# Attention and a gated feed-forward in one planned kernel: the weight loads behind the first forty go in single file

## The chip, the cores and the metric

The kernel runs on one core of a Trainium2 chip. The metric is the device time of one execution in microseconds (us); times are given as the median of the executions shown.

## What is computed

The reference has two parts, and the second reads the first's output.

```
B, H, S, D = 8, 8, 576, 64                       # attention, for every batch b and head h
q_d, k_d, v_d = means of q, k, v over groups of 4 positions      # 144 positions
out_up    = repeat(softmax(q_d k_d^T / 8) v_d, 4 times each)
out_local = softmax(q k^T / 8, only where |i - j| < 4) v
x = (out_up + out_local) as 4608 tokens x 512
h = x @ w_in            # 512 x 2048
y = (h * cos(h)) @ w_out    # 2048 x 512
```

All data is float32 at the interface. The weights come as 64-bit floats and are turned into pairs of 32-bit floats (a high and a low part) on the chip.

## The kernel before

**Work and tiles.** Attention is done in units of one batch and two heads: b0 to b7, four units each. A unit has loads of q and k (`u_qk`, L478) and of v in two layouts, vd and vl (`u_v`, L498), then scores and softmax (`u_s`), transposes (`u_t`) and the product with v (`u_pv`), which writes one of four ring slots of x tiles (x0 to x3). The feed-forward goes over 12 tiles of 384 tokens and 16 slices of 128 of the inner width. A step is one tile and one slice: `gemm1` (L946, 12 matmuls at L969 of 384 columns), an epilogue on ACT, DVE and POOL (L978 to L987) and, two steps later, `gemm2` (L991, nine matmuls at L1005 of 512 columns). The epilogue holds one of two PSUM banks until its second pass on DVE (L984) is through. The first three tiles go through the slices in three passes: slices 0 to 3, then 4 to 7, then 8 to 15, three tiles in each; the other nine tiles go through all 16 slices at once. Steps are numbered from 0 in that order: steps 0 to 11 are the first pass, 12 to 23 the second, 24 to 47 the third. So slice 4 is first needed at step 12, and slice 15 at step 31.

**Weights.** For each slice there are two loads of 512 KB: wdi (a slice of w_in) and wdo (a slice of w_out), made by `w_load` (L407) on SP's queue. A loaded slice is split (`w_split`, L417): an absolute value on ACT (L425), four passes on DVE (L426 to L432), a cast to the high part on ACT or DVE (L436, L437) and a subtraction on POOL or DVE (L404). The buffers of slices 6 to 15 hold data of the first attention units before that (names beginning with wxi and wxo), so those loads wait until the units are through.

**What sets the order.** Every operation is recorded in a plan with an engine, a cost and its dependencies; some have a choice of engines. A list scheduler (`Plan.run`, L163) goes over the recorded operations eight times forwards and backwards with priorities, keeps the best outcome, and the operations are then issued to each engine's in-order queue in the order of their planned starts. The loads of the first units and of all weights are tied to one order (L1069 to L1072). A load's planned cost is its size by a rate on SP and 1.8 more until it is there (L396). The planner also puts fillers into TensorE's order before 300 us of its plan (L1131: a 128x512 matmul on a constant, into an unused bank), where it expects TensorE to wait or to be too little busy.

**Loads in flight.** `dma` (L388) gives each of the first forty transfers on SP's queue (FIRST = 40) a wait for the transfer three ahead of it (AHEAD = 3), so that three are in flight. Behind the fortieth there is no such wait. Each SP transfer uses one of eight semaphores in turn (DMAHW0 to DMAHW7), and waits for the earlier transfer with the same one; besides, it waits for the engines that use its buffer. SP's queue also carries the output stores of the first three tiles' first passes (L1027) and small moves of softmax results (ptb, L854), all in order. An output store reads a buffer ob, which shares a ring of four with the epilogue's tiles tr.

Of the kernel before, what the change touches and what calls it, by code (L numbers as in the profile page):

```python
# [24 lines left out]
P = 128  # L25
# [9 lines left out]
NF = 4  # L35
# [15 lines left out]
ON_PE = ()  # L51
BOOST = {0: 100.0}
LAG = 2
AHEAD, FIRST = 3, 40
PI = math.pi


# [223 lines left out]
def _mmr(n, k=1):  # L281
    return k * n * 0.0004543
# [6 lines left out]
def _act(n, psum=True, extra=0):  # L289
    return n * 0.000833 + (0.051 if psum else 0.093) + 0.093 * extra  # L290


def _dve(n):
    return n * 0.001042 + 0.065
# [7 lines left out]
def attn_ffn_kernel(ctx: ExitStack, tc: tile.TileContext, qT, kT, vdn, vl, w_in, w_out, out):  # L302
    nc = tc.nc
    pe, act, dve, pool, sp = nc.tensor, nc.scalar, nc.vector, nc.gpsimd, nc.sync
# [6 lines left out]
    pl = Plan()  # L311

    def sb(tag, n, shape, dtype=F32, name=None, pool=None):
        t = pl.turn(tag, n)
        return pl.buf(lambda: (pool or ap).tile(shape, dtype, name=name or tag, tag=t, bufs=1), t)

    def psum(tag):
        pl.banks.append((tag, pl.buf(lambda: ps.tile([P, 512], F32, name="bank", tag=tag, bufs=1), tag)))
        return pl.banks[-1][1]
# [65 lines left out]

    loads, begun = {}, []

    def dma(nbytes, fn, r=(), w=(), pw=()):  # L388
        def begin():
            ins = fn()  # L390
            if ins is not None and len(begun) < FIRST:
                if len(begun) >= AHEAD:
                    tc.add_manual_dep(ins.ins, begun[-AHEAD].name, mybir.DependencyInfo(
                        mybir.DependencyClass.Sync, mybir.DependencyReason.DATA), reason="loads in flight")
                begun.append(ins.ins)
        o = pl.op("SP", max(0.45, nbytes / 262e3), begin, r=r, w=w, pw=pw, lat=1.8)  # L396
        loads.setdefault((pl.name,) + pl.arg, []).append(o)
        return o

# [7 lines left out]
    def w_load(k, c):  # L407
        pl.name = "w_load"
        wd = words[(k, c)]
        if k == "i":  # L410
            src = lambda: w_dram["i"][:, :, c * P:(c + 1) * P, :]
            dst = lambda: wd.get().rearrange("p (a f) t -> p a f t", a=KC)
        else:
            src, dst = (lambda: w_dram["o"][c * P:(c + 1) * P]), wd.get
        dma(4096 * P, lambda: sp.dma_start(dst(), src()), w=[wd])
# [535 lines left out]
    def pe_order(o):  # L951

        if prev[0] is not None:
            o.sdeps.append(prev[0])
        prev[0] = o
# [35 lines left out]
    po, part = {}, {}  # L991

    def gemm2(t, c, c0, c1):
        pl.name = "gemm2"
        gh, gl = gt.pop((t, c))
        if c == c0:
            po[t] = [psum(f"po.{i}") for i in range(SIZE[t] // P)]
        wo, accs = wgt[("o", c)], po[t]
        end = (t, c) == (NT - 1, NC - 1)

        def mm(i, lo, hi):
            sl = slice(i * P, (i + 1) * P)
            o = accs[i].get()
            for k in range(lo, hi):
                pe.matmul(o, (gh, gh, gl)[k].get()[:, sl], wo.get()[:, (0, 1, 0)[k]], start=(c == c0 and k == 0),  # L1005
                          stop=(c == c1 - 1 and k == 2))

        def high(i):
            pe_order(pl.op("PE", 2 * _mmr(DM), lambda: mm(i, 0, 2), r=[gh, wo], w=[accs[i]]))
        if end:  # L1010
            high(0)
            high(1)
        for i in range(SIZE[t] // P):
            lo = 2 if end else 0
            if end and i == 2:
                high(2)
            pe_order(pl.op("PE", (3 - lo) * _mmr(DM), lambda i=i: mm(i, lo, 3), r=[gh, gl, wo], w=[accs[i]]))
            if c == c1 - 1:
                bk, ob = accs[i], sb("tr", 4, [P, DM], name="ob", pool=fp)

                pl.op("ACT", _act(DM), lambda bk=bk, ob=ob: act.activation(ob.get(), bk.get(), AF.Copy, scale=-4.0 * PI),
                      r=[bk], w=[ob], alts=[("DVE", _dve(DM), lambda bk=bk, ob=ob: dve.tensor_scalar(
                          out=ob.get(), in0=bk.get(), scalar1=-4.0 * PI, scalar2=None, op0=ALU.mult))])
                dst = out[FROM[t] + i * P:FROM[t] + (i + 1) * P, :]
                if c0 == 0:
                    part[(t, i)] = pl.buf(None)
                    dma(2048 * P, lambda dst=dst, ob=ob: sp.dma_start(dst, ob.get()), r=[ob], w=[part[(t, i)]])  # L1027
                else:

                    pl.op("POOL", 1.0, lambda dst=dst, ob=ob: pool.dma_start(dst, ob.get(), accum_op=ALU.add),  # L1030
                          r=[ob], w=[part[(t, i)]], lat=2.5)
# [22 lines left out]
    for c in range(NC):  # L1054
        for k, d in (("i", 0.0), ("o", 0.7)):
            t = need[c]
# [73 lines left out]
    def wide(s):  # L1130
        return pe.matmul(s[2].get(), ident_b, ident_b.unsqueeze(1).broadcast_to([P, 4, P]), start=True, stop=True)  # L1131
# [5 lines left out]
    with tc.manual_schedule():  # L1137
        constants()
        for o in order:
            if o.eng == "PE" and o.start < CFG["fend"]:  # L1140
# [3 lines left out]
                if s:  # L1144
# [5 lines left out]
                    for (x, d), (y, _) in zip(marks, marks[1:] + [(o.start - 0.2, None)]):  # L1150
                        n = int((y - x) * CFG["fill"] / 0.22)
                        if y > o.start - 0.3:
                            n = max(n, least)
                        for i in range(n):
                            ins = wide(s)
# [51 lines left out]
```

## Time and profile before

| | us |
|---|---|
| three timed executions | 999.63, 1001.82, 1000.99 |
| their median | 1000.99 |
| the profiled execution, whole | 1007.59 |
| its span, first to last instruction | 1005.80 |
| TensorE busy in it | 988.6 |
| VectorE busy in it | 677.0 |
| ScalarE busy in it | 612.3 |
| mean share of the DMA engines | 0.27 of the span |

The profiled execution lies 6.60 us above the median of the timed ones; 1.79 us of it lie outside the span. In the profile's rows PE is TensorE's matmul side, DVE is VectorE, ACT is ScalarE, POOL is GpSimd, and SPq is the queue of SyncE. A row of the timeline has its start, its length, engine, line, operation, tiles and count, and in square brackets the idle time before it and what ended it. A window row has the stretch, then for PE, PEld, DVE, ACT and POOL the busy time and the instructions, then TensorE's granted clock, the DMA engines' share and GB/s.

### The profile page before, as it was taken

To read this page: it belongs to the slowest core of one execution; us is meant where nothing else is said; L and a number is where in the kernel's file an instruction comes from. 1 tells how busy PE (TensorE), PEld (TensorE's weight loads), DVE (VectorE), ACT (ScalarE), POOL (GpSimd) and SP (SyncE) were. 2 spreads that over 40 slices of the span, in tenths; PEclk is the share of its full clock that TensorE was granted. 3 is DMA by queue.
4 is the path that set the end of the run, shared out by engine and by line. 5 is a ranking of instruction groups with operands and counts; after the bars stand their busy time and mean duration, and the time that the engine had idled before them with its cause. 6 is when DMAs were issued, how large, how long until landed. Compare 5 with 4: busy or idle time off the path is not lost.

```text
span 1005.8 us, 24165 instructions
## 1 busy us (share of the span) xinstructions
PE 988.6 (98%) x10081; PEld 858.6 (85%) x10081; DVE 677.0 (67%) x1418; ACT 612.3 (61%) x1175; POOL 185.6 (18%) x250
## 2 busy tenths in 40 slices
PE   7999999999999999999999999999999999999998
PEld 4767888998888888889888888888888888899997
DVE  5489989997778668464758867655657875433433
ACT  2349868886567656555547756655646755655554
POOL 3257325352232103000002111100001200000000
PEclk9599999999999999999999999999999999999999
DMA  7861663224243412210212412201112320100000
GB/s 233 251 216 38 222 236 98 43 33 92 61 104 96 92 50 72 67 33 28 80 50 69 129 49 57 83 25 37 62 54 72 113 63 3 38 1 1 32 1 32
DMA packets 39756, 78.36 MB, mean 78 GB/s; under 512 B 4832, under 2 KB 16096, under 8 KB 39648
## 3 DMA queue, kind: packets, MB, share of 16 engines
q1 hardware_dynamic: 37056, 72.11, 22.9%
q0 software_dynamic: 2592, 4.72, 3.3%
q8 instruction: 79, 1.29, 0.5%
q14 instruction: 29, 0.24, 0.1%
HBM read 57.93 MB, written 14.16 MB: 72 GB/s over the span
## 4 chain that ended last, share of the span: by engine, by line
PE 89%; DVE 4%; issue 3%; DMA 2%; ACT 1%; SPq 1%; POOL 0%; ACTq 0%; DVEq 0%; POOLq 0%
PE bank L969 37%; PE bank L1005 37%; PE bank L1131 2%; PE bank L731 2%; PE bank L914 2%; PE bank L750 2%; PE bank L895 1%; PE bank L890 1%; PE bank L867 1%; DMA q<-qT 1%; PE bank L907 1%; DMA ptb<-sml 1%; PE bank L864 1%; PE bank L676 1%; SPq L854 1%
## 5 line engine op out<-in xcount | busy, mean ns | idle before, releaser
L1005 PE MATMUL bank<-wo,gh 128*128 128x512 f32 x1152 | 364.3, 397 | 0.0
L1005 PEld LDWEIGHTS bank<-wo,gh 128*128 128x128 f32 x1152 | 209.4, 188 | 38.3 <-issue 3.6
L1005 PE MATMUL bank<-wo,gl 128*128 128x512 f32 x576 | 227.5, 395 | 0.0
L980 ACT ACTIVATE tr<-bank,bmagic 128x384 f32<-128x384 f32 x192 | 111.0, 578 | 108.7 <-PE bank L969 104.0
L984 DVE SCALAR_TENSOR_TENSOR tr<-tr,bank 128x384 f32<-128x384 f32 x192 | 105.0, 547 | 105.2 <-ACT tr L979 104.3
L981 DVE SCALAR_TENSOR_TENSOR tr<-tr,bank 128x384 f32<-128x384 f32 x192 | 105.5, 550 | 82.5 <-ACT tr L980 81.3
L978 ACT ACTIVATE tr<-tr 128x384 f32<-128x384 f32 x192 | 100.5, 523 | 81.8 <-DVE tr L981 81.3
L986 ACT ACTIVATE gh<-tr 128x384 fp32r<-128x384 f32 x160 | 83.7, 523 | 88.2 <-DVE tr L984 86.7
L404 DVE TENSOR_TENSOR gl<-tr,gh 128x384 fp32r<-128x384 f32 x159 | 95.5, 601 | 57.9 <-ACT gh L986 55.6
L1005 PEld LDWEIGHTS bank<-wo,gl 128*128 128x128 f32 x576 | 108.0, 188 | 23.5
L969 PE MATMUL bank<-x1h,wi 128*128 128x384 f32 x384 | 107.4, 340 | 0.8 <-DVE tr L984 0.8
L969 PE MATMUL bank<-x0h,wi 128*128 128x384 f32 x384 | 107.0, 339 | 0.0
L969 PE MATMUL bank<-x2h,wi 128*128 128x384 f32 x384 | 106.8, 339 | 0.0
L969 PE MATMUL bank<-x3h,wi 128*128 128x384 f32 x384 | 106.5, 338 | 0.0
L979 ACT ACTIVATE tr<-tr 128x384 f32<-128x384 f32 x192 | 100.9, 525 | 6.1
L404 POOL TENSOR_TENSOR gl<-tr,gh 128x384 fp32r<-128x384 f32 x33 | 38.4, 1165 | 233.2 <-DVE gh L987 150.2
L969 PEld LDWEIGHTS bank<-x1h,wi 128*128 128x128 f32 x384 | 70.2, 188 | 3.7 <-DVE tr L984 1.6
L969 PEld LDWEIGHTS bank<-x0h,wi 128*128 128x128 f32 x384 | 70.2, 188 | 2.1
L969 PEld LDWEIGHTS bank<-x2h,wi 128*128 128x128 f32 x384 | 70.2, 188 | 2.0 <-issue 0.2
L969 PEld LDWEIGHTS bank<-x3h,wi 128*128 128x128 f32 x384 | 70.2, 188 | 2.0
L969 PE MATMUL bank<-x3l,wi 128*128 128x384 f32 x192 | 64.5, 336 | 0.0
L969 PE MATMUL bank<-x0l,wi 128*128 128x384 f32 x192 | 64.5, 336 | 0.0
(277 smaller groups left out, 1436.7 us busy)
## 6 DMA issues: line engine op xcount, KB each, us to landing
vl<-vl SPq DMA_DIRECT2D x26, 384.0 KB, 3.0
out<-ob SPq DMA_DIRECT2D x36, 256.0 KB, 2.1
wdi<-w_in SPq DMA_DIRECT2D x16, 512.0 KB, 10.2
wdo<-w_out SPq DMA_DIRECT2D x16, 512.0 KB, 6.8
q<-qT SPq DMA_DIRECT2D x26, 292.0 KB, 3.5
k<-kT SPq DMA_DIRECT2D x26, 292.0 KB, 3.1
vd<-vdn SPq DMA_DIRECT2D x26, 288.0 KB
out<-ob POOLq DMA_DIRECT2D x18, 256.0 KB, 5.0
```

The costliest lines, as they stand in the source:

```text
L404: f = lambda e: lambda: e.tensor_tensor(out=out(), in0=in0(), in1=in1(), op=ALU.subtract)
L731: pe.matmul(banks[h].get()[BS * g:BS * (g + 1), c:c + BS], q.get()[hs, o:o + BS], k.get()[hs, o:o + BS], start=True, stop=True)
L750: pe.matmul(banks[h].get()[:HD, i * SD:(i + 1) * SD], qkd.get()[hs, 0, i * HD:(i + 1) * HD], qkd.get()[hs, 1, :], start=True, stop=True)
L914: pe.matmul(banks[e].get()[64 * h:64 * h + 64, o:o + 2 * BQ], v4[r, NSEG * h + n, :], pt[r, :, NSEG * h + n, :BQ], start=True, stop=True)
L969: pe.matmul(ph.get()[:, :m], w[:, i, kc, :], x[:, kc, :], start=(n == 0), stop=(n == 3 * KC - 1))
L978: act.activation(tr.get(), tr.get(), AF.Sin, scale=PI)
L979: return act.activation(tr.get(), tr.get(), AF.Square)
L980: pl.op("ACT", _act(m, True, 1), lambda: act.activation(tr.get(), h(), AF.Identity, bias=bmagic), r=[ph], w=[tr])
L981: pl.op("DVE", _dve(m), lambda: dve.scalar_tensor_tensor(out=tr.get(), in0=tr.get(), scalar=MAGIC, in1=h(), op0=ALU.subtract, op1=ALU.subt ...
L984: pl.op("DVE", _dve(m), lambda: dve.scalar_tensor_tensor(out=tr.get(), in0=tr.get(), scalar=0.5, in1=h(), op0=ALU.subtract, op1=ALU.mult), ...
L986: pl.op("ACT", _act(m, False), lambda: act.activation(gh.get(), tr.get(), AF.Copy), r=[tr], w=[gh], alts=[("DVE", _dve(m / 2), lambda: dve ...
L1005: pe.matmul(o, (gh, gh, gl)[k].get()[:, sl], wo.get()[:, (0, 1, 0)[k]], start=(c == c0 and k == 0), stop=(c == c1 - 1 and k == 2))
```

## The change

Loads 41 to 80 on SP's queue now wait for the one load directly ahead of them, in place of none; output stores are neither counted nor given a wait, and no load waits for them. In the planner a weight load of slice 4 or higher now occupies SP for its transfer and the 1.8 that stood behind it, so that the plan has these loads one behind the other too.

```
-AHEAD, FIRST = 3, 40
+AHEAD, FIRST, LAST = 3, 40, 80
...
-    def dma(nbytes, fn, r=(), w=(), pw=()):
+    def dma(nbytes, fn, r=(), w=(), pw=(), load=True):
         def begin():
             ins = fn()
-            if ins is not None and len(begun) < FIRST:
-                if len(begun) >= AHEAD:
-                    tc.add_manual_dep(ins.ins, begun[-AHEAD].name, mybir.DependencyInfo(
+            if ins is not None and load and len(begun) < LAST:
+                n = AHEAD if len(begun) < FIRST else 1
+                if len(begun) >= n:
+                    tc.add_manual_dep(ins.ins, begun[-n].name, mybir.DependencyInfo(
                         mybir.DependencyClass.Sync, mybir.DependencyReason.DATA), reason="loads in flight")
                 begun.append(ins.ins)
-        o = pl.op("SP", max(0.45, nbytes / 262e3), begin, r=r, w=w, pw=pw, lat=1.8)
+        alone = pl.name == "w_load" and pl.arg[1] >= NF
+        o = pl.op("SP", max(0.45, nbytes / 262e3) + 1.8 * alone, begin, r=r, w=w, pw=pw, lat=1.8 * (not alone))
...
-                    dma(2048 * P, lambda dst=dst, ob=ob: sp.dma_start(dst, ob.get()), r=[ob], w=[part[(t, i)]])
+                    dma(2048 * P, lambda dst=dst, ob=ob: sp.dma_start(dst, ob.get()), r=[ob], w=[part[(t, i)]], load=False)
```

Behind `dma` the line numbers of the changed kernel are higher by two. Since the planner sees other costs, the orders of all engines change in the stretch up to about step 48. Three places follow.

On SP, before, the stretch from the store of the first tile's second block to the loads of slice 11; wdo6 is slice 6 of w_out, and the names in brackets are what the transfer waits for:

```order
L1027 DMA out<-ob_1817 128x512 [waits DMAHW3_49,DVE_49]
L415 DMA wdo6_1878<-w_out 128x1024 [waits DMAHW4_49,PE_49]
L415 DMA wdi7_1908<-w_in 128x4x256
L1027 DMA out<-ob_1910 128x512 [waits DMAHW6_49,DVE_49]
L415 DMA wdo7_1940<-w_out 128x1024 [waits DMAHW7_49]
L415 DMA wdi8_2004<-w_in 128x4x256 [waits DMAHW0_49,Pool_49]
L415 DMA wdo8_2021<-w_out 128x1024 [waits DMAHW1_49]
L415 DMA wdi9_2074<-w_in 128x4x256 [waits DMAHW2_49]
L415 DMA wdo9_2095<-w_out 128x1024 [waits DMAHW3_49]
L415 DMA wdi10_2172<-w_in 128x4x256 [waits DMAHW4_49,DVE_49,Activation_49]
L415 DMA wdo10_2180<-w_out 128x1024 [waits DMAHW5_49]
L415 DMA wdi11_2210<-w_in 128x4x256 [waits DMAHW6_49,PE_49]
```

The same stretch on SP now:

```order
L1029 DMA out<-ob_1873 128x512 [waits Activation_49]
L417 DMA wdo6_1910<-w_out 128x1024 [waits DMAHW1_49,PE_49]
L1029 DMA out<-ob_1912 128x512 [waits Activation_49]
L417 DMA wdi7_1993<-w_in 128x4x256 [waits DMAHW4_49]
L417 DMA wdo7_2068<-w_out 128x1024 [waits DMAHW6_49]
L417 DMA wdi8_2155<-w_in 128x4x256 [waits DMAHW7_49,DVE_49,Pool_49]
L417 DMA wdo8_2187<-w_out 128x1024 [waits DMAHW0_49]
L417 DMA wdi9_2223<-w_in 128x4x256 [waits DMAHW2_49,DMAHW1_49]
L1029 DMA out<-ob_2236 128x512 [waits DMAHW3_49,Activation_49]
L1029 DMA out<-ob_2258 128x512 [waits Activation_49]
L1029 DMA out<-ob_2261 128x512 [waits DMAHW5_49,Activation_49]
L417 DMA wdo9_2309<-w_out 128x1024 [waits DMAHW2_49]
```

Each load now waits for the semaphore of the load ahead of it, where it waited for a transfer eight places back, and the three stores of the second tile stand behind wdi9, where they stood behind wdo11.

On PE, before, the end of step 5's gemm1 and what follows it; wo3 is the high and low part of w_out's slice 3, and L665 and L676 are matmuls of an attention unit of b1:

```order
L969 MATMUL bank_1738<-x1l_674,wi1_1117 128x384
L969 MATMUL bank_1738<-x1h_673,wi1_1117 128x384
L1005 MATMUL bank_1358<-wo3_1734,gh_1721 128x512 x2
L1005 MATMUL bank_1358<-wo3_1734,gl_1752 128x512
L665 MATMUL bank_1769<-wxo10_140 64x96 x4
L1005 MATMUL bank_1364<-wo3_1734,gh_1721 128x512 x2
L1005 MATMUL bank_1364<-wo3_1734,gl_1752 128x512
```

The same place on PE now:

```order
L971 MATMUL bank_1729<-x1h_672,wi1_1123 128x384
L648 MATMUL bank_1757<-wxi10_136 72x96 x4
L1007 MATMUL bank_1421<-wo3_1748,gh_1725 128x512 x2
L1007 MATMUL bank_1421<-wo3_1748,gl_1755 128x512
L1133 LDWEIGHTS ident_b_73
L1133 MATMUL bank_1757<-ident_b_73 128x512
L1133 LDWEIGHTS ident_b_73
L1133 MATMUL bank_1757<-ident_b_73 128x512
L1133 LDWEIGHTS ident_b_73
L1133 MATMUL bank_1757<-ident_b_73 128x512
L1133 LDWEIGHTS ident_b_73
L1133 MATMUL bank_1757<-ident_b_73 128x512
```

Four fillers now stand ahead of the unit's matmuls (L667 in the new numbering). In all there are 89 fillers where there were 81: 70 ahead of step 1 as before, 12 ahead of step 2 (9 before), 2 ahead of step 3 and none ahead of step 4 (none and 2 before), 4 ahead of step 6 (none before), and one ahead of step 22 (none before). The steps themselves keep their order.

On DVE, before, what stands between the second epilogue passes (L984) of steps 16 and 17; xxh is the buffer of a split in work, and gl the low part of an epilogue:

```order
L984 SCALAR_TENSOR_TENSOR tr_2548<-tr_2548,bank_2525 128x384
L426 TENSOR_SCALAR xxh_507<-xxh_507 128x512
L404 TENSOR_TENSOR gl_2591<-tr_2548,gh_2586 128x384
L428 TENSOR_SCALAR xxh_507<-xxh_507 128x512 x2
L981 SCALAR_TENSOR_TENSOR tr_2595<-tr_2595,bank_2569 128x384
L430 SCALAR_TENSOR_TENSOR xxh_507<-wdo9_2095,xxh_507 128x512
L430 SCALAR_TENSOR_TENSOR xxh_507<-wdi10_2172,xxh_507 128x512
L984 SCALAR_TENSOR_TENSOR tr_2595<-tr_2595,bank_2569 128x384
```

The same place on DVE now:

```order
L986 SCALAR_TENSOR_TENSOR tr_2540<-tr_2540,bank_2513 128x384
L783 TENSOR_REDUCE mxl_2577<-sml_2394 128x12
L434 SCALAR_TENSOR_TENSOR xxh_507<-wdo9_2309,xxh_507 128x512
L983 SCALAR_TENSOR_TENSOR tr_2585<-tr_2585,bank_2554 128x384
L428 TENSOR_SCALAR xxh_507<-xxh_507 128x512
L1024 TENSOR_SCALAR ob_2618<-bank_2462 128x512
L790 TENSOR_REDUCE mxd_2623<-bank_2097 72x2
L986 SCALAR_TENSOR_TENSOR tr_2585<-tr_2585,bank_2554 128x384
```

A copy of an output block (L1024) that ACT made before, and two pieces of the first b2 unit's softmax (L783, L790) that stood behind step 20 before, now stand between these two epilogues. Counted from the second epilogue pass of step 7 to that of step 20, DVE has 106 instructions where it had 95. Ahead of step 0's it has 145 where it had 136, and from there to step 7's 104 where it had 112.

## The prediction

> **What bounds the kernel now.** The page comes first, with its busy times and its chain of waits.
>
> ```profile
> span 1005.8 us, 24165 instructions
> PE 988.6 (98%) x10081; PEld 858.6 (85%) x10081; DVE 677.0 (67%) x1418; ACT 612.3 (61%) x1175; POOL 185.6 (18%) x250
> PE 89%; DVE 4%; issue 3%; DMA 2%; ACT 1%; SPq 1%; POOL 0%; ACTq 0%; DVEq 0%; POOLq 0%
> ```
>
> TensorE is the bound, 89% of the chain. But a share over the whole span hides the stretch that the change touches, so the second view is the windows, by stage (PE, PEld, DVE, ACT, POOL busy, then clock, DMA share, GB/s).
>
> ```profile
> 62.00:80.00 18.00, 16.32 (x267) 10.89 (x265) 17.49 (x50) 10.83 (x31) 11.52 (x16) 1.00 0.67 229
> 80.00:125.00 45.00, 44.86 (x877) 36.85 (x878) 42.84 (x106) 40.47 (x85) 25.85 (x33) 1.00 0.43 139
> 125.00:130.00 5.00, 3.04 (x67) 2.70 (x54) 3.89 (x10) 0.83 (x2) 0.00 (x0) 1.00 0.94 338
> 130.00:165.00 35.00, 34.66 (x174) 31.08 (x174) 33.36 (x55) 28.14 (x54) 12.75 (x12) 1.00 0.52 184
> 165.00:235.00 70.00, 70.00 (x405) 62.98 (x404) 65.66 (x122) 56.11 (x106) 27.99 (x26) 1.00 0.25 38
> 300.00:1005.00 705.00, 699.92 (x6515) 619.26 (x6512) 431.07 (x892) 414.08 (x755) 69.10 (x89) 1.00 0.18 53
> ```
>
> From 80 us on TensorE is busy nearly without a gap, with one exception between 125 and 130 us. VectorE is the second bound: idle 1.64 us of 35 and 4.34 of 70, where the weights are split. Behind 300 us it is idle 39% of the time. Whatever the change does must therefore show before about 235 us as an earlier or later TensorE; behind that it is only carried along.
>
> The exception, from PE's timeline, and the engine's own account of all its matmuls of that line:
>
> ```profile
> 124.21 1.13 PE L731 MATMUL bank<-k,q 64*32 64x32 f32 x88
> 127.30 0.27 PE L731 MATMUL bank<-k,q 64*32 64x32 f32 x8 [1.96 <-issue]
> L731 PE MATMUL bank<-k,q 64*32 64x32 f32 x2304 | 25.3, 196 | 2.0 <-issue 2.0
> ```
>
> In the middle of 96 small matmuls TensorE stands still for 1.96 us and waits for nothing that the profile shows. The line has 24 units of 96 matmuls, and this is the only stall of it on PE. It falls at the end of the heaviest burst of loads, 0.94 of the DMA engines and 338 GB/s. The burst begins on SP's queue:
>
> ```profile
> 110.52 0.34 SPq L415 DMA_DIRECT2D wdo<-w_out  x1
> 110.91 0.43 SPq L415 DMA_DIRECT2D wdi<-w_in  x1
> 120.58 1.34 SPq L415 DMA_DIRECT2D wdo<-w_out  x1
> 155.94 0.38 SPq L415 DMA_DIRECT2D wdo<-w_out  x1
> ```
>
> Eleven weight loads go out from 110.52 (wdo6) to 120.58 (wdo11). The last weight load, wdo15, goes out at 155.94.
>
> **The change, part by part. The loads in single file.** No row shows one 512 KB load alone. These rows bound it:
>
> ```profile
> vl<-vl SPq DMA_DIRECT2D x1, 384.0 KB, 3.0
> wdo<-w_out SPq DMA_DIRECT2D x4, 512.0 KB, 7.3
> ```
>
> Alone in its stretch (80 to 105 us), 384 KB took 3.0 us from issue to landing; in the burst 512 KB took 7.3, with up to seven others. The lower end is 3.0, the upper 7.3. I take 4.0, the quiet row scaled by 512/384, and 0.4 for the issue: 4.4 per load, since in single file nothing else fills the DMA engines. From wdo6 on there are 19 weight loads, which gives 19 x 4.4 = 83.6 us. The splits wait for them; their first pass on ACT began, for wdi7, wdi11 and wdo15:
>
> ```profile
> 138.07 0.67 ACT L425 ACTIVATE xxh<-wdi 128x512 f32<-128x512 f32 x1
> 175.31 0.68 ACT L425 ACTIVATE xxh<-wdi 128x512 f32<-128x512 f32 x1 [0.52 <-POOL wo L404]
> 215.89 0.67 ACT L425 ACTIVATE xxh<-wdo 128x512 f32<-128x512 f32 x1
> 136.05 2.48 SPq L1027 DMA_DIRECT2D out<-ob  x3
> 153.05 2.80 SPq L1027 DMA_DIRECT2D out<-ob  x3
> ```
>
> If wdo6 again goes out at 110.5 (it waits for TensorE's use of its buffer), wdi7 lands at 119.3, 19 us ahead of its split. Five loads later the queue stands at 132.5 and meets the second tile's stores, whose data was there at 136.05; they end at 138.5. Three loads later it is 151.7, and the third tile's stores hold it until about 155. The ten left end at 199, 17 us ahead of wdo15's split. So the loads stay hidden, at a cost of nothing; the cover is gone when a load takes over 6.1 us ((215.9 - 155)/10). The stores, the only other thing queued behind a waiting load, come up while the queue waits for their data, so the ring of four that they free is not held longer.
>
> **The burst goes, and the stall with it?** One load at a time can't reach 0.94 of the DMA engines. If the burst delays TensorE's next instructions, 1.96 us go; if not, nothing. I take -1.96 for TensorE's own path, because one stalled unit of 24, in the burst, is hardly chance. The instructions come by DMA too:
>
> ```profile
> q8 instruction: 79, 1.29, 0.5%
> ```
>
> That is 79 packets of 16 KB on a queue of their own. The Trainium skill, DMA: Bandwidth & Descriptors, section Queues, rings and completion order, says that each DMA engine takes turns between the queues that have work, a packet at a time. By that rule a burst on q1 could delay q8 only by a packet or so, and the stall would be no matter of the burst and would stay; the sum would be without the -1.96. The place of the stall speaks against it, but no row shows a fetch waiting.
>
> **The fillers.** Eight more. The three ahead of step 2 and two ahead of step 3 stand about where TensorE waits for VectorE (62 to 80 us: VectorE 17.49 of 18), against two that go ahead of step 4; they cost nothing there. The four ahead of step 6 stand in the stretch where TensorE had no idle time. Their pace:
>
> ```profile
> 58.98 2.76 PE L1131 MATMUL bank<-ident_b 128*128 128x512 bf16 x12
> ```
>
> 0.23 us each, 0.92 for four: between 0, if the unit's matmuls behind them wait anyway, and +0.92. I take +0.5.
>
> **VectorE is late next.** Where the stall was, VectorE waited too, and behind it TensorE waited for VectorE once (the matmul of step 16):
>
> ```profile
> 131.16 0.55 DVE L981 SCALAR_TENSOR_TENSOR tr<-tr,bank 128x384 f32<-128x384 f32 x1 [2.27 <-ACT tr L980]
> PE bank L969 <- DVE tr L984: 0.3, 1, 0.3
> ```
>
> So around 162 us the two engines are level. VectorE's new order has more between the second epilogue passes of steps 7 and 20. The prices, from the groups of 125 to 240 us:
>
> ```profile
> L1022 DVE TENSOR_SCALAR ob<-bank 128x512 f32<-128x512 f32 x2 | 1.4, 688 | 0.2 <-PE bank L1005 0.2
> L987 DVE CAST gh<-tr 128x384 fp32r<-128x384 f32 x2 | 0.7, 354 | 0.1
> L778 DVE TENSOR_TENSOR sml<-bank,band 128x192 f32<-128x192 f32 x2 | 0.6, 351 | 0.0
> L781 DVE TENSOR_REDUCE mxl<-sml 128x12 f32<-128x384 f32 x1 | 0.5, 547 | 0.0
> L788 DVE TENSOR_REDUCE mxd<-bank 72x2 f32<-72x288 f32 x2 | 0.8, 444 | 0.0
> L791 DVE TENSOR_TENSOR smd<-bank,mxd 72x288 f32<-72x288 f32 x2 | 0.8, 442 | 0.0
> L816 DVE TENSOR_REDUCE su<-sml 128x12 f32<-128x384 f32 x1 | 0.5, 541 | 0.0
> L404 DVE TENSOR_TENSOR gl<-tr,gh 128x384 fp32r<-128x384 f32 x18 | 13.6, 753 | 0.6 <-ACT gh L986 0.5
> L404 DVE TENSOR_TENSOR wi<-xxh,wi 128x512 fp32r<-128x512 f32 x5 | 3.4, 682 | 0.0
> L404 DVE TENSOR_TENSOR x2l<-wxi,x2h 128x384 fp32r<-128x384 f32 x1 | 0.5, 549 | 0.0
> L428 DVE TENSOR_SCALAR xxh<-xxh 128x512 int32<-128x512 int32 x22 | 9.9, 458 | 0.0
> L432 DVE SCALAR_TENSOR_TENSOR xxh<-wdi,xxh 128x512 int32<-128x512 int32 x11 | 7.5, 681 | 0.0
> ```
>
> Added: three output copies (2.06), a gh cast (0.35), two weight casts (no row of before has one; 0.354 x 512/384 = 0.47 each, 0.94; not below the 0.35 of the smaller gh cast), seven softmax pieces of the first b2 unit (two L778, one L781, two L788, two L791: 3.02) and one L816 (0.54): 6.91. The net of the splits: two L432 more (1.36), and gone are two gl (1.51), one wi (0.68), one x2l (0.55), one L428 (0.46): -1.84. Sum +5.1. Against it stands what VectorE left idle: 1.11 (125 to 130), 1.64 (130 to 165) and 18/70 of 4.34 up to 183 us: 3.9. So VectorE comes to step 20 about 1.2 us later than before, although TensorE alone could be 1.96 earlier: the later of the two counts, and the stall's time is not won. The ends: -1.5, if the pieces moved forward fill idle time and hold no epilogue (then TensorE's -1.96 + 0.5 decides), and +2.8, if only the stall's own 2.27 can be filled. The planner's new filler ahead of step 22 shows that its plan too has TensorE waiting there. What left that stretch is done behind step 20, where it frees VectorE but gives TensorE nothing back.
>
> **The early order.** Nine more VectorE instructions ahead of step 0's epilogue and eight fewer up to step 7's. Before 62 us VectorE was idle often, in 62 to 80 it held TensorE; TensorE's part there was 18 - 16.32 = 1.68 us idle, most of it behind VectorE. Between 0 and -1.7; since the fillers stay, I take -0.5.
>
> **The sum.** +1.2 (VectorE, in place of the stall) + 0.5 (fillers) - 0.5 (early order) = +1.2 us. Against the profiled execution's 1007.59 (span 1005.80 and 1.79 around it) that is 1008.8; against the median of the timed executions, 1000.99, which lies 6.6 lower, 1002.2. About 0.2% (2.0 us) is what a measurement of this kernel can tell from no change, so this is no change.
>
> **Rivals.** *The stall goes and nothing takes its place.* VectorE's pieces find idle time, and the early order gives its 1.7: -1.96 + 0.5 - 1.7 = -3.2, 997.8. For it: most moved pieces are short, and VectorE was idle for 3.9 of the 58 us from 125 to 183; against: step 16 already waited for VectorE. *VectorE holds TensorE fully.* In steps 14 to 20 nothing but the stall's idle can be filled, since the rest is waiting for ACT between two passes of one epilogue: +2.8 + 0.9 and no early gain: +3.7, 1004.7. It decides over the forecast from the point where under 3 of VectorE's 3.9 idle us are usable; small, so this rival is close. *The stall stays*, since the burst was not its cause: then its 2.27 us idle can't be filled either, 5.1 - 1.6 = +3.5, 1004.5 at the most. The rule of turns in the Trainium skill's page DMA: Bandwidth & Descriptors leads there. *Loads too late*, on the same side: at 7.3 each, the ten behind 155 us end at 228, 12 us behind their split, and TensorE would wait most of it, 1012. It decides from 6.1 per load; the 3.0 of the quiet row speaks against it. That the change doesn't do what it says is ruled out by the order: each of these loads names the semaphore of the one ahead.
>
> **Chances and range.** Forecast 0.39. Stall gone and time won 0.27. VectorE holding TensorE 0.21, stall staying 0.10, loads late 0.03. So faster 0.27, same 0.39, slower 0.34. The forecast alone would be 999.0 to 1003.0. The range that leaves out 2 in 10 goes to the first rival's 997.8 and somewhat below for the unpriced early order, and above 1004.7 by the fillers and the weight casts: 997.0 to 1006.5.
>
> **What would show it.** Right: no stall at L731 near step 8, DMA share behind 110 us near half and never over 0.9, loads landing 3.5 to 4.5 us apart, wdo15 landed by 205 us, VectorE over 95% busy from step 8 to 20 and one or two TensorE waits for L986 there, together 1 to 3 us; then every later step 1 us later. Wrong: a load spacing over 6 us, a stall at the same L731, a TensorE without waits up to step 24, or a difference that arises behind 300 us.

## The result

| | us |
|---|---|
| kernel before, median of 22 executions | 1000.06 |
| changed kernel, median of 22 executions | 1005.53 |
| ratio, with its 95% interval | 1.0062 [1.0041, 1.0083] |
| changed kernel, the profiled execution, whole | 1003.26 |
| its span | 1001.5 |

The change makes the kernel about 0.6% slower, 5.5 us by the medians, where 1.2 us were forecast and called no change. The medians are of all executions shown; the ratios and their intervals, here and below, leave out those that were disturbed.

**The profile after.** The page of the changed kernel, with the span, the busy times and the chain of waits:

```profile
span 1001.5 us, 24178 instructions
PE 984.2 (98%) x10089; PEld 852.9 (85%) x10089; DVE 678.3 (68%) x1423; ACT 605.7 (60%) x1167; POOL 189.3 (19%) x254
PE 87%; DMA 6%; DVE 3%; POOL 1%; issue 1%; ACT 1%; SPq 1%; ACTq 0%; DVEq 0%; POOLq 0%
```

DMA, 2% of the chain before, is 6% now, and issue is down from 3% to 1%: two percentages to look behind. The span is *shorter* than the 1005.80 of before, although the kernel is slower. That is the clock in the first 60 us, which differs from profile to profile (last section): the profile of before had TensorE at 0.50 for some 20 us there, this one for 3 us. Spans of single profiles therefore can't be compared here. What can is the distance between steps, from step 6 on, where both run at full clock. The table takes the start of the first gemm1 matmul of a step from PE's timeline, in a second profile of the kernel before (the first experiment), in the changed kernel, and in two experiments that follow:

| step | before, again | changed | changed, less before | chain to 69, less before | pairs free, less before |
|---|---|---|---|---|---|
| 7 | 112.72 | 107.41 | -5.31 | -2.41 | -5.06 |
| 8 | 122.94 | 115.97 | -6.97 | -4.07 | -6.71 |
| 19 | 169.50 | 162.11 | -7.39 | -4.49 | -7.13 |
| 32 | 224.46 | 220.76 | -3.70 | -1.52 | -4.89 |
| 36 | 244.68 | 240.99 | -3.69 | -1.52 | -4.88 |
| 38 | 256.30 | 255.96 | -0.34 | -1.04 | -5.35 |
| 52 | 332.75 | 334.44 | +1.69 | -0.29 | -5.36 |

Read down a column: only its changes count. The changed kernel wins 1.66 at step 7 to 8 (the stall), 0.42 up to step 19, loses 3.69 between steps 19 and 32, 3.35 between 36 and 38 and 2.03 between 38 and 52. Together +7.0 from step 7 to 52. The last 2.03 are not the change's alone: they lie at steps 42 to 43 and 51 to 52, where TensorE waits for moves of softmax results (ptb), and the first profile of the kernel before lost 1.1 us more than the second at the same place (its longest such wait is 1.32 us, the second's 0.40). In the changed kernel:

```profile
330.93 0.31 PE L916 MATMUL bank<-ptb,vl 64*64 64x48 f32 x2 [1.85 <-DMA ptb<-sml]
```

The waits of TensorE in the changed kernel between 60 and 320 us (line waited at, what ended it, us in total, times, longest):

```profile
PE bank L971 <- DVE tr L986: 2.9, 3, 1.4
PE bank L648 <- POOL qkd L541: 1.2, 1, 1.2
PE bank L869 <- DVE smd L834: 0.9, 1, 0.9
PE bank L916 <- DMA ptb<-sml: 0.8, 1, 0.8
PE bank L1007 <- DVE wo L406: 0.6, 1, 0.6
PE bank L1007 <- DVE gl L406: 0.4, 1, 0.4
```

The stall "issue" at the small matmuls (L731 before, L733 now) is not in the list. Four of the six rows name VectorE instead. SP's timeline shows the loads in single file:

```profile
111.64 0.38 SPq L417 DMA_DIRECT2D wdi<-w_in  x1
115.46 0.33 SPq L417 DMA_DIRECT2D wdo<-w_out  x1
119.33 0.38 SPq L417 DMA_DIRECT2D wdi<-w_in  x1
...
178.02 0.33 SPq L417 DMA_DIRECT2D wdo<-w_out  x1
...
234.06 0.34 SPq L483 DMA_DIRECT2D q<-qT  x1
239.91 0.33 SPq L483 DMA_DIRECT2D k<-kT  x1
```

From one begin to the next it is 3.8 to 3.9 us in the first three rows, over the whole file 3.3 to 3.9 where nothing else holds the queue, and the last weight load, wdo15, goes out at 178.02. But the file does not end there: q and k of a b2 unit, at 234 and 240 us, are loads 74 and 75 of the 80, and k begins 5.85 us behind q. The pair before it, loads 70 and 71, goes out at 183.94 and 186.72. The profile's chain leads from that k over GpSimd's sums, a weight's subtraction, ScalarE's absolute value and VectorE's gl to a wait of TensorE at step 28, the first gemm1 matmul of which is

```profile
202.69 0.44 PE L971 MATMUL bank<-x0h,wi 128*128 128x384 f32 x1 [0.48 <-DVE tr L986]
```

The step starts 0.65 us late by it, which it does not in the two experiments of the table. What the later pair does on VectorE and on TensorE, from their timelines (start, length, instruction, idle time before it and who ended it), and the clock by windows of 2 us (the number third from the right):

```profile
242.84 0.75 DVE L497 TENSOR_REDUCE qkd<-k 128x144 f32<-128x576 f32 x1 [4.28 <-DMA k<-kT]
243.51 0.55 DVE L406 TENSOR_TENSOR gl<-tr,gh 128x384 fp32r<-128x384 f32 x1
```

```profile
244.12 0.51 PE L1007 MATMUL bank<-wo,gl 128*128 128x512 f32 x1 [0.40 <-DVE gl L406]
246.95 0.66 PE L869 MATMUL bank<-ident,smd 72*72 72x72 f32 x8 [0.94 <-DVE smd L834]
248.60 0.69 PE L971 MATMUL bank<-x1h,wi 128*128 128x384 f32 x1 [0.99 <-DVE tr L986]
```

```profile
246.00:248.00 2.00, 0.67 (x9) 0.52 (x8) 1.24 (x3) 1.19 (x3) 1.45 (x2) 1.00 0.00 0
248.00:250.00 2.00, 1.40 (x4) 1.40 (x5) 1.57 (x4) 1.42 (x4) 0.00 (x0) 0.57 0.12 30
250.00:252.00 2.00, 2.00 (x8) 2.00 (x8) 1.10 (x3) 0.63 (x2) 0.00 (x0) 0.58 0.27 73
```

VectorE stands 4.28 us before the k of the next unit; the second profile of before has a wait of 2.07 us for such a load there, but with gl already done. Behind that instruction in its queue are the low part gl that gemm2 needs, the softmax (smd) that the transposes need and the epilogue (tr) that frees the bank for gemm1. TensorE waits for each in turn, 2.33 us in three pieces, and then runs 4 us at little over half its clock, some 1.7 us more (4.0 x 0.43). Less the one wait of 0.8 that the second profile of before has there, that is 3.2 of the 3.35 between steps 36 and 38.

### The profile page after: what moved, and what is told of

It is laid out like the page before. It is cut to its first block, busy times and chain, and to the rows that moved or that the text cites. A ratio compares the mean times of both kernels' runs of the same rounds, so it can differ in the third digit from the quotient of the medians.

```text
span 1001.5 us, 24178 instructions
## 1 busy us (share of the span) xinstructions
PE 984.2 (98%) x10089; PEld 852.9 (85%) x10089; DVE 678.3 (68%) x1423; ACT 605.7 (60%) x1167; POOL 189.3 (19%) x254
## 4 chain that ended last, share of the span: by engine, by line
PE 87%; DMA 6%; DVE 3%; POOL 1%; issue 1%; ACT 1%; SPq 1%; ACTq 0%; DVEq 0%; POOLq 0%
PE bank L971 36%; PE bank L1007 36%; PE bank L733 2%; PE bank L916 2%; PE bank L1133 2%; DMA q<-qT 2%; PE bank L752 2%; DMA wdo<-w_out 2%; PE bank L897 1%; DMA wdi<-w_in 1%; PE bank L869 1%; DMA k<-kT 1%; PE bank L892 1%; DMA ptb<-sml 1%; SPq L856 1%
## 5 line engine op out<-in xcount | busy, mean ns | idle before, releaser
L1007 PE MATMUL bank<-wo,gh 128*128 128x512 f32 x1152 | 364.9, 398 | 0.6 <-DVE wo L406 0.6
L1007 PEld LDWEIGHTS bank<-wo,gh 128*128 128x128 f32 x1152 | 209.5, 188 | 39.1 <-issue 3.6
L1007 PE MATMUL bank<-wo,gl 128*128 128x512 f32 x576 | 227.5, 395 | 0.4 <-DVE gl L406 0.4
L986 DVE SCALAR_TENSOR_TENSOR tr<-tr,bank 128x384 f32<-128x384 f32 x192 | 104.9, 546 | 103.2 <-ACT tr L981 102.2
L1007 PEld LDWEIGHTS bank<-wo,gl 128*128 128x128 f32 x576 | 108.0, 188 | 24.4 <-DVE gl L406 0.8
L971 PE MATMUL bank<-x1l,wi 128*128 128x384 f32 x192 | 65.0, 338 | 0.0
```

Source lines behind the costliest of these rows:

```text
L971: pe.matmul(ph.get()[:, :m], w[:, i, kc, :], x[:, kc, :], start=(n == 0), stop=(n == 3 * KC - 1))
L986: pl.op("DVE", _dve(m), lambda: dve.scalar_tensor_tensor(out=tr.get(), in0=tr.get(), scalar=0.5, in1=h(), op0=ALU.subtract, op1=ALU.mult), ...
```

## The experiments

Two things were changed together: the order of all engines (the planner's cost `alone`) and the waits (the chain, `LAST`). So they were taken apart, in all four combinations, and then the chain by its parts. All ratios are to the kernel before, on the same chip; the medians come from several chips, so two rows are best compared by their ratios.

| kernel | order | in flight behind the fortieth | median us | ratio, 95% interval |
|---|---|---|---|---|
| before, again | old | no limit | 998.65 | 0.9987 [0.9958, 1.0016] |
| changed | new | 1 to load 80 | 1005.53 | 1.0062 [1.0041, 1.0083] |
| order only | new | no limit | 999.41 | 0.9990 [0.9963, 1.0016] |
| waits only | old | 1 to load 80 | 1029.92 | 1.0314 [1.0277, 1.0351] |
| chain to 69 | new | 1 to load 69 | 1000.64 | 1.0003 [0.9973, 1.0032] |
| tail only | new | 1 for loads 70 to 80 | 1005.83 | 1.0045 [1.0011, 1.0079] |
| stores on GpSimd | old | 1 to load 69 | 1026.03 | 1.0245 [1.0212, 1.0277] |
| two from the start | new | 1 to load 69, and 2 among the first forty | 1010.25 | 1.0088 [1.0062, 1.0115] |
| two behind | old | 2 to load 69 | 997.51 | 0.9955 [0.9923, 0.9987] |
| pairs free | new | 1 to load 69, then 2 to 80 | 998.65 | 0.9976 [0.9944, 1.0007] |
| three behind | old | 3 to load 69 | 996.34 | 0.9959 [0.9928, 0.9991] |

**The theory at the start.** Two causes: the new order (VectorE late) and the end of the chain (the b2 loads); against it the waits alone, the order alone, and the clock of the first 60 us.

### The kernel before, again

No edit.

> The kernel before, unchanged, for a second profile and for the granted clock of each of its runs. In the changed kernel's runs the time goes with the clock, 998.2 us of span at 0.998 and 1001.5 at 0.995, about 1 us for 0.001. Theory of two causes (new order and the end of the chain, nothing of the clock at the start): ratio 1.00 and, at the same granted clock, about 5.5 us below the changed kernel, so a span near 996 at 0.995. Rival, the clock at the start: the two lie on one line, and the kernel before is quicker only since its clock is higher, about 0.999 in most runs. In the second profile the stall of about 2 us in a softmax unit's small matmuls near step 8 comes again if the burst makes it.

At the same granted clock it does lie below the changed kernel: 995.4 us of span at 0.995 in one run, where the changed kernel had 1001.5. So the clock of the start is not the cause of the difference. The second profile has the burst and the stall again, by windows of 5 us and on PE's timeline:

```profile
115.00:120.00 5.00, 5.00 (x132) 4.04 (x131) 4.94 (x8) 4.40 (x10) 2.08 (x2) 1.00 1.04 372
120.00:125.00 5.00, 3.49 (x97) 3.15 (x84) 4.15 (x10) 1.09 (x2) 0.00 (x0) 1.00 0.95 340
```

```profile
122.11 0.27 PE L731 MATMUL bank<-k,q 64*32 64x32 f32 x8 [1.51 <-issue]
```

And on its SP queue the pair of the b2 unit goes out together:

```profile
237.76 0.34 SPq L481 DMA_DIRECT2D k<-kT  x1
238.16 0.76 SPq L481 DMA_DIRECT2D q<-qT  x1
```

### The order alone

```
-AHEAD, FIRST, LAST = 3, 40, 80
+AHEAD, FIRST, LAST = 3, 40, 40
```

> The new order of all engines, with no load behind the fortieth waiting for another (LAST = 40). From the two traces, step by step: the new order loses about 3 us ahead of step 6 and 3.7 between steps 19 and 32, where VectorE comes late; the chain wins 2.1 at the stall and loses 3.7 at step 37, where one of a pair of b2 loads waits for the other. Theory of two causes: the loss at step 37 goes and the stall comes back, 1005.5 - 3.7 + 2.1 = 1003.9, ratio 1.004. Rival, the waits alone: 1000.1, ratio 1.000. Rival, the order alone: 1005.5, ratio 1.0055.

999.41, ratio 0.9990: not the theory's number, but the first rival's, that the order costs nothing. The half of my theory that charged the new order with several us falls. Its trace shows why the loss at VectorE does not add up to one: reckoned as in the table it lies 12.65 us behind the kernel before at step 7 (its first 66 us ran at half clock for long) and 14.11 at step 32, so 1.5 are lost in between, which the interval, up to +1.6, just allows; and the stall, which it was expected to have in full, is small, though no load waits:

```profile
PE bank L971 <- DVE tr L986: 2.4, 2, 1.4
...
PE bank L733 <- issue: 0.3, 1, 0.3
```

In the new order six loads begin together near step 7 (the planner put stores between them), where eleven did in the old one.

### The waits alone

```
-        alone = pl.name == "w_load" and pl.arg[1] >= NF
+        alone = False
```

This gives the old order word for word on every engine, with the chain.

> The old order of all engines, with loads 41 to 80 each waiting for the one ahead (the planner's cost is left as before). Theory of two causes: the stall of 2.1 goes, and the pair of b2 loads near step 37 goes one behind the other and costs up to 3.7: 1000.1 - 2.1 + 3.7 = 1001.7, ratio 1.0016. Rival, the waits alone: 1005.5, ratio 1.0055. Rival, the order alone: 1000.1 with the stall still there, or 998.0 with it gone.

1029.92: no theory had it. The rows that carry it, from all engines' waits between 100 and 200 us and SP's timeline:

```profile
ACT tr L982 <- DMA out<-ob: 19.4, 2, 11.0
POOL qkd L490 <- DMA q<-qT: 17.8, 1, 17.8
...
PE bank L1007 <- ACT gh L988: 15.4, 2, 8.6
```

```profile
144.53 0.33 SPq L417 DMA_DIRECT2D wdo<-w_out  x1
144.91 1.44 SPq L1029 DMA_DIRECT2D out<-ob  x3
```

The output stores have no wait of the chain, but they stand on SP's in-order queue. In the old order the second tile's three stores come behind wdo11, and wdo11 now begins only at 144.53; in the second profile of the kernel before the same stores began at 130.84. Until they are done their ring of four is full, ScalarE can't start an epilogue (19.4 us in two waits), and TensorE stands. By steps: 11.7 us are lost at step 13, 8.5 at step 17 and 4.3 at steps 19 and 20; 6.0 at step 5, where v, k and q loads of b2 are late: GpSimd has their sums ahead of the low part x1l, TensorE waits 2.65 us for that and then runs at little over half its clock for some 7 us. So the stall's 1.7 are won here too (step 8), and the chain without the planner's knowledge of it costs 30.

This run has one more answer. The pair of b2 loads is in single file here too, k at 262.65 and q at 267.05, yet between steps 36 and 38 this kernel loses only 0.07 us where the changed one loses 3.35. On VectorE:

```profile
267.35 0.81 DVE L406 TENSOR_TENSOR gl<-tr,gh 128x384 fp32r<-128x384 f32 x1
270.00 0.75 DVE L497 TENSOR_REDUCE qkd<-q 128x144 f32<-128x576 f32 x1 [1.84 <-DMA q<-qT]
```

Counted from the start of step 35 the sum over the second load begins at 4.6 us, in the second profile of before at 4.5, in the changed kernel at 6.1: here the second load went out 4.40 us behind the first, not 5.85, and once out it landed within 3 us. Besides, gl stands ahead of the sum here and behind it there. So a pair in single file need not cost anything; it costs where the second load lands later than the two together would have. How much of the difference is the earlier load and how much the place of gl, no run separates.

### The chain to load 69

```
-AHEAD, FIRST, LAST = 3, 40, 80
+AHEAD, FIRST, LAST = 3, 40, 69
```

> The changed kernel with the chain ended at the sixty-ninth load, wdo15, so that the eleven b2 loads behind it begin freely. Theory of two causes: the waits at steps 36 to 38 (0.40, 0.94 and 0.99 us in the changed kernel) and the low clock right behind them go, 1005.5 - 3.7 = 1001.8, ratio 1.0017. Rival, the order alone: 1005.5, ratio 1.0055, since VectorE comes late at step 37 in any case.

1000.64, ratio 1.0003: the theory's number within 1.2 us; the rival's 1005.5 is outside of the interval. In the trace the pair goes out together again, VectorE waits 2.54 us for its k in place of 4.28, and TensorE's waits at L869 and for gl at L1007 are gone:

```profile
236.24 0.35 SPq L483 DMA_DIRECT2D q<-qT  x1
236.65 0.86 SPq L483 DMA_DIRECT2D k<-kT  x1
```

### The tail alone

```
-                if len(begun) >= n:
+                if len(begun) >= n and not FIRST <= len(begun) < 69:
```

> The new order, with only loads 70 to 80 in single file (the eleven b2 loads behind wdo15); the weight loads 41 to 69 begin freely. Theory: the end of the chain is a cause by itself. Against the kernel with the new order and no chain (999.4) this one gets the waits at steps 28, 36 to 38 and 43 and the low clock behind them, 4.9 us from the two traces: 1004.3, ratio 1.0045. Rival: the b2 loads are late only because the weight loads ahead of them are late; then 999.4, ratio 0.999.

Ratio 1.0045, as expected of the tail in the new order. Against the order alone it is 5.5 us by the ratios (6.4 by the medians, from two chips). Its trace, at half clock for most of the first 68 us and read behind them, has the wait for smd again (PE bank L869, 0.9 us), and k begins 5.13 us behind q (259.03 and 253.90). Between steps 36 and 38 it loses 2.7 us against the kernel before. The rival, that the weight loads must be late first, falls.

### The stores on GpSimd's queue

In the old order with the chain to load 69:

```
-                    dma(2048 * P, lambda dst=dst, ob=ob: sp.dma_start(dst, ob.get()), r=[ob], w=[part[(t, i)]], load=False)
+                    dma(2048 * P, lambda dst=dst, ob=ob: pool.dma_start(dst, ob.get()), r=[ob], w=[part[(t, i)]], load=False)
```

> The old order, weight loads in single file to wdo15 (the sixty-ninth), and the output stores on GpSimd's queue in place of SP's. Theory: the 30 us of the old order with the chain come from the stores that stand behind single-file loads on SP's in-order queue (the second tile's began 14 us later than in the kernel before, and ScalarE waited 19 us for them). Off that queue they are on time: 25 us go, and the stall of 1.5 to 2 is gone too, 1000 - 2 = 998, ratio 0.998. Rival: the weight loads themselves come too late for the old order's splits; then most of the 30 stays, over 1015.

1026.03. By the total the theory fell; by the steps half of it stands. From step 8 to 18 this kernel keeps pace with the kernel before to 0.03 us, so the 20 us at steps 13 and 17 were the stores. But at step 5 it loses 8.9 us (6.0 in the waits-only kernel), and at step 19 20.8 us at one stroke:

```profile
POOL qkd L490 <- DMA q<-qT: 26.7, 1, 26.7
ACT xxh L427 <- POOL wi L406: 23.1, 2, 21.8
...
PE bank L1007 <- ACT ob L1023: 18.8, 1, 18.8
```

GpSimd's in-order queue has, in the old order, the sums over q of the second b2 unit ahead of a weight's subtraction. That q stands behind wdo15 on SP and goes out at 177 us, not at 151. GpSimd waits 26.7 us for it, ScalarE for GpSimd, TensorE for ScalarE. In the waits-only kernel the same wait lay mostly in the shadow of the stores (4.3 us). It is neither "the stores" nor "the splits come too late for their weights": it is everything that was queued behind the loads, one thing hidden by the other.

### Two in flight from the start

```
-AHEAD, FIRST, LAST = 3, 40, 80
+AHEAD, FIRST, LAST = 2, 40, 69
```

> The changed kernel with the chain ended at the sixty-ninth load, and with two instead of three loads in flight among the first forty. Theory: what spreads the runs of one kernel over 20 us is TensorE standing still at 11 to 25 us with the DMA engines 0.8 to 1.0 busy, and the granted clock of 0.50 that follows for 4 to 44 us; with fewer loads in flight these stalls and the low clock get rarer, granted clock 0.998 in most runs and none under 0.98. The time then is 995 to 1000, unless the first loads come later: rival, step 0 is held by its loads, and starts 5 to 10 us later than the 48.1 of the kernel with three in flight; 1005 to 1010.

1010.25: the rival. Step 0 starts at 51.2, but step 1 at 69.6, 18.4 us later instead of 12.8 in the chain to 69, as the first units' loads are late. The chain of its profile runs over loads nearly without a break from 30 to 65 us. The granted clock did not improve: its median is 0.9925, where 0.998 was expected, so that part of the theory falls. In this profile the half clock, from 59 us on, comes behind waits of 1.71 and 2.16 us for ScalarE and VectorE, so the run doesn't decide what the stalls of the first 25 us do.

### Two in flight behind the fortieth

In the old order, with the chain to load 69:

```
-                n = AHEAD if len(begun) < FIRST else 1
+                n = AHEAD if len(begun) < FIRST else 2
```

> The old order, with two loads in flight instead of one behind the fortieth, to the sixty-ninth. At 3.6 us a load, two in flight need 1.8 us a load: the eleven loads from wdo6 at 105.8 are through SP's queue by 126, ahead of the second tile's stores at 130.8, so nothing of the 30 us is left. Theory: it is the burst of eleven at once that stalls TensorE near step 8; with two in flight the stall goes, 1000.0 - 1.9 = 998, ratio 0.998. Rival: any busy DMA engines will do, the stall stays, 1000, ratio 1.000.

997.51, ratio 0.9955 [0.9923, 0.9987]: 0.45% below the kernel before, and below the changed one. The stall is 0.2 us, the second tile's stores go out as soon as their data is there (129.13), and step 8 comes 1.3 us sooner behind step 7 than in the kernel before. A second gain of 1.0 at step 37 was not expected: the wait of 0.79 us for VectorE's tr that the kernel before has there is not in its trace; why is not shown.

### The pairs free

```
-                n = AHEAD if len(begun) < FIRST else 1
+                n = AHEAD if len(begun) < FIRST else 1 if len(begun) < 69 else 2
```

> The changed kernel with two instead of one in flight for the eleven b2 loads at the end of the chain (loads 70 to 80); the weight loads stay in single file. Theory: what costs the 4.9 us is that the second of a pair of q and k loads waits for the first (5.85 us at step 34 of the changed kernel), not that these loads carry a wait at all; with two in flight a pair goes together, 1005.5 - 4.9 = 1000.6, ratio 1.0005. Rival: any wait on the earlier loads delays them, and it stays at 1005, ratio 1.005.

998.65, ratio 0.9976 [0.9944, 1.0007]: the chain may go to load 80, as long as the second of a pair doesn't wait for the first. In the trace q and k of the later pair leave 0.4 us apart (232.88 and 233.28), and steps 36 to 38 lose nothing (-4.88 to -5.35 in the table).

### Three in flight behind the fortieth

In the old order, with the chain to load 69:

```
-                n = AHEAD if len(begun) < FIRST else 1
+                n = AHEAD
```

> The old order, three loads in flight behind the fortieth (as among the first forty), to the sixty-ninth. With one in flight the DMA engines were 0.29 to 0.70 busy near step 7 and TensorE did not stall, with two 0.68 to 0.81 and 0.2 us, with all at once 0.94 to 1.04 and 1.5 to 2.0 us. Theory: the stall comes with saturated DMA engines; three in flight keep them at 0.8 to 0.95, as they do ahead of 60 us, and the stall is between, 0.2 to 1.0 us: 998 to 999.5, ratio 0.998. Rival: it comes from the length of the queue, eleven loads deep; then three in flight do as well as two, ratio 0.9955.

Ratio 0.9959 [0.9928, 0.9991], as good as two. The theory that full DMA engines stall TensorE falls, since they are full here and PE does not stop:

```profile
105.00:110.00 5.00, 5.00 (x94) 4.31 (x93) 4.91 (x15) 3.20 (x9) 2.15 (x4) 1.00 0.95 310
110.00:115.00 5.00, 5.00 (x94) 4.25 (x92) 4.94 (x8) 4.39 (x10) 2.67 (x2) 1.00 0.98 317
115.00:120.00 5.00, 5.00 (x122) 4.39 (x121) 4.88 (x13) 2.41 (x5) 0.00 (x0) 1.00 0.92 317
```

What goes with the stall is the number of loads begun close together: eleven, 1.5 and 2.0 us; six (the order alone), 0.3; one to three in flight, 0.2 or none. The six come in another order of all engines, so that number is the weakest of these.

## Why the prediction was right and wrong

The number fell within the range by luck: 1005.53 lies near its upper end, for a reason that the range did not have in it. The forecast itself, no change, did not hold, since the interval of the ratio leaves out 1.

**The loads in single file: the size near, the count wrong.** 4.4 us a load were forecast, and 3.3 to 3.9 came. wdo15 began at 178 us and no weight load of the file held TensorE, as forecast (the one wait for a split weight, 0.6 us, comes before wdo6 and is there without any chain, 0.8 in the order alone); with the chain ended there the kernel is at 1.0003. The step that failed is "So the loads stay hidden, at a cost of nothing": I counted 19 loads from wdo6 to wdo15 and stopped, although the chain goes on for eleven more, which belong to b2's units. Six of them are pairs of q and k that used to go together (the others are loads of v), and whoever sums over them has the next epilogue behind it in its queue. This missing term is 5.9 us by the ratios against the chain to 69 (1.0062 and 1.0003) and 4.9 by the table of steps (+7.0 and +2.1 from step 7 to 52); it is as large as the whole result. Against the pairs free it is 8.6 by the ratios, but the intervals of these two kernels overlap.

It is no fixed price of the wait: the old order with the same chain loses 0.07 us between steps 36 and 38, since its second load landed in time. Most of it lies at 244 to 252 us, so "must therefore show before about 235 us" failed with it: an idle VectorE did not mean a VectorE without a due time.

The count did not begin at the forty-first load either: ten loads of the file stand ahead of wdo6, among them q and k of the first b2 unit. TensorE's wait of 1.2 us for GpSimd's qkd in the list above goes back to that q, and is not there with no load in file (the order alone); what it is worth by itself no run shows.

**Held only by the plan.** "The stores, the only other thing queued behind a waiting load" was wrong too: the second b2 unit's q and k stand there. The changed kernel pays only the 0.65 us at step 28 for it, since its planner knew what a load costs and moved the stores and sums. In the old order the same waits cost 30 us. This was the rival of loads too late, with another price and another place, and I had let it hang on the splits alone.

**The stall.** Forecast -1.96, measured -1.66 against the second profile of before; with a limit on the weight loads it is 0.2 us or less, in both orders. The rule that I set against it, that each DMA engine takes turns between the queues with work (the Trainium skill, DMA: Bandwidth & Descriptors, Queues, rings and completion order), would have had it stay. It went. With three in flight, at 0.92 to 0.98 of the DMA engines, there is none, so full engines alone don't do it, and that much agrees with the rule. Why the stall comes with eleven loads begun close together, no run here shows.

**VectorE late.** Forecast one or two waits for L986 around step 20, +1.2 net of the stall, bounds -1.5 and +2.8. The wait came, at step 22, for the epilogue of step 20. TensorE, VectorE and ScalarE there:

```profile
176.84 0.44 PE L971 MATMUL bank<-x2h,wi 128*128 128x384 f32 x1 [1.41 <-DVE tr L986]
```

```profile
175.19 0.68 DVE L1024 TENSOR_SCALAR ob<-bank 128x512 f32<-128x512 f32 x1
175.79 0.53 DVE L818 TENSOR_REDUCE su<-sml 128x12 f32<-128x384 f32 x1
176.25 0.54 DVE L986 SCALAR_TENSOR_TENSOR tr<-tr,bank 128x384 f32<-128x384 f32 x1
```

```profile
169.78 1.28 ACT L813 ACT_TABLE_LOAD   x1
...
172.66 1.28 ACT L980 ACT_TABLE_LOAD   x1
```

The output copy (L1024) and the sum (L818) that the prediction had listed stand right ahead of it. VectorE was 98% busy from step 8 to 21 (53.66 of 54.88 us), as forecast. What the prediction had not listed are ScalarE's two loads of function tables around the softmax that moved forward, 2.56 us in the same epilogue. From step 7 to 32 the kernels with the new order and a chain to 69 or free pairs come out 0.9 and 0.2 us behind the kernel before, and the changed kernel 1.6, of which 0.65 is step 28. So the term was right, a little under its forecast.

**The fillers and the early order** can't be told apart from the clock of the first 60 us. The order alone, at 0.9990 [0.9963, 1.0016], says that all of the new order together lies between 0.4% faster and 0.2% slower.

**The rivals.** The time of "VectorE holds TensorE fully" (1004.7) is near, and its cause, VectorE's extra work in steps 14 to 20, was not at work: with the pairs free the same extra work is done and the kernel is at 998.65, ratio 0.9976. Of "the stall goes and nothing takes its place" the first half came true, 1.66 us at step 8, and the second did not; the whole describes the old order with two or three in flight.

## What to carry to other kernels

A wait put on "the loads" falls on every load that the counter reaches: go to the last one that it covers, and ask of each who waits for it and what stands behind that waiter in its in-order queue, and whether the load then lands later than it did: 1.5 us (6.1 against 4.5) cost 3.4 here, and the same wait in the other order cost nothing. To take the edge off a burst, limit it to two or three in flight; single file cost 30 us in an order that was not planned for it, and won no more at the stall. And compare profiles step by step behind the point where their clocks agree, not by their spans.

## What the runs showed of the hardware

**Behind a short stop TensorE's granted clock can be at half for long.** In the second profile of the kernel before, PE's timeline and windows of 4 us:

```profile
11.18 0.47 PE L750 MATMUL bank<-wxi 64*72 64x144 f32 x4 [1.32 <-issue]
...
21.07 1.20 PE L890 MATMUL bank<-ptd,vd 72*64 72x144 f32 x15 [1.14 <-issue]
```

```profile
20.00:24.00 4.00, 2.92 (x19) 1.36 (x18) 2.25 (x8) 2.60 (x11) 0.00 (x0) 0.78 0.87 228
24.00:28.00 4.00, 4.00 (x107) 3.80 (x108) 1.17 (x3) 0.00 (x1) 0.00 (x0) 0.50 0.77 226
...
36.00:40.00 4.00, 4.00 (x36) 3.59 (x33) 0.02 (x1) 0.29 (x1) 0.00 (x0) 0.50 0.74 218
```

The stop of 1.14 us is followed by some 20 us at 0.50, in the profile of the order alone one of 1.41 us at the same place by 44 us. In the changed kernel the stop there was 0.22 us, and the clock stayed at 1.00. But the length of a stop alone does not decide: the one of 1.32 us ten us earlier left the clock at 1.00 (the windows from 8 to 20 us), and one of 1.61 us at that place in the changed kernel was followed by some 3 us at 0.50. What decides, no run here shows. Most of the difference between these profiles lies there, which is why a span of one profile can mislead by 10 us; for executions without a trace only the mean clock is known, and in the changed kernel the time went with it, from 998.2 us of span at 0.998 to 1017.8 at 0.978.

The Trainium skill, TensorE: Matmul & The Clock Gate, Part 1, puts the half rate after an idle window of about 3.4 us and the full rate after about as long of work. Here shorter stops were followed by it, and it lasted through 16 us in which the rows have TensorE busy without a gap; the 4 us at 248 to 252 in the changed kernel, in dense large matmuls, agree with the page's second number. Why it lasted so much longer in the first case, no run here shows.
